# Retention attention with a soft mixture of experts on one core: other first loads, an earlier start of the scores of steps 2 and 3, and another last dispatch

## The chip, the cores and the metric

The kernel runs on one core of one Trainium2 chip. The metric is the device time of one execution in microseconds (us). Before the change it is 166.42 us, the median of three runs (166.32 to 166.59). All data are 32-bit floats, and a 32-bit product on TensorE shows in the trace as two instructions, a transpose as one.

## The reference

Two stages follow each other.

```
attention, per batch b (4) and head h (8), over 768 tokens t, head size 64:
    state = gamma[h] * state + outer(k[t], v[t])
    y[t]  = (q[t] @ state) / sqrt(64)
x = y as [3072 tokens, 512]
logits    = x @ phi                                  # 32 slots, 4 for each of 8 experts
d         = softmax of logits over the TOKENS        # dispatch
slot_in   = d.T @ x                                  # [32, 512]
slot_out  = relu(slot_in[e] @ w1[e]) @ w2[e]         # per expert, hidden size 1024
c         = softmax of logits over the SLOTS         # combine
out       = c @ slot_out
```

The dispatch softmax runs over all 3072 tokens, so no expert can begin before the attention of every token is done.

## The kernel before

**Work units.** The 768 tokens of a batch are cut in 6 chunks of 128. A step is one chunk of one batch: 24 steps, numbered chunk by chunk, step `i` belonging to batch `i % 4`. Two steps make a pair `P` (12 pairs), four steps make a group `g` (6 groups). The state recurrence is written by chunks: inside a step `score_mm` forms k·q for the 8 heads (16 products), `score_mask` (VectorE, one instruction for each of two PSUM banks) masks it into a tile A, and `attend_mm` multiplies it with v. `carry_mm` adds what the running state gives, `state_mm` and `state_add` bring the state forward. The decay factors are multiplied into q and v by GpSimd (`decay_q`, `decay_v`). The first four steps have no earlier state: they skip `carry_mm` and `decay_q`.

**Per pair.** `attend_mm` writes a pair's outputs in banks Y0 and Y1, each holding half of the heads of both steps. `attend_copy` takes them to memory as yT (Y0 by ScalarE, Y1 by VectorE; 128x512 each). `natural_mm` transposes yT (8 transposes), `natural_copy` brings the result to a tile xn. `logits_mm` multiplies yT with phi.

**Per group.** `logits` takes the maximum over the tokens so far and exponentiates; `turn_mm` transposes; `dispatch_u` multiplies the weights with xn, and `dispatch_acc` adds the product to `acc` with the factor `al` for a risen maximum, and to the sum `zrun`. `combine_a`, `combine_b`, `split_c`, `transpose_c` and `copy_c` prepare c.

**The last group** stands apart: its logits have a maximum of their own, and its product `u` is copied by ScalarE (four 128x128 copies), not added to `acc`. Two factors per slot (`wj`, two columns) then bring both to one scale, and the slot inputs `sp` are two rows of four products: one with `acc` (L511), one with `u` (L517). `siT` (L520) is what `hidden` (L533), the first expert product, reads.

**Order and queues.** Every engine executes its instructions in the order in which the program lists them. All transfers are issued by SyncE's queue in order. An input step is one transfer of 1024 KB (k, q, v and k again in token order), but steps 0 and 1 come in three parts: k and q (512 KB), v (256 KB), and k in token order as a late part (256 KB). Steps 0 to 5 are loaded ahead, step `i + 6` when the slot of step `i` is free, that is after `state_mm` of its pair.

**Weights.** 32 weight tiles of 1024 KB go between the inputs by `PACE`. 13 slots of their own and the 6 input slots hold 19 of them. The twentieth waits until `hidden(0, 0)` has used up the first tiles. Twelve output tiles of 512 KB end the program.

**PSUM.** The banks have names: A0 to A3, Y0, Y1, S and sm. `warm` issues products of zeros.

The start, as the program lists it for TensorE (lines 410 to 468): 5 `warm`, `score_mm(0)`, 4 `warm`, `attend_mm(0, [0])`, `score_mm(1)`, 2 `warm`, then pair 0: `attend_mm(0, (1,))`, `state_mm(0)`, `natural_mm(0)`, `score_mm(2)`, `score_mm(3)`, then pair 1: `attend_mm(1)`, `state_mm(1)`, and so on.

Of the kernel before, what the change touches and what calls it, by code (L numbers as in the profile page):

```python
# [80 lines left out]
def retention_soft_moe_kernel(  # L81
# [42 lines left out]
    wsel = small("wsel", [128, 2, NSLOT])  # L124
# [88 lines left out]
    def carry_mm(P):  # L213
        p = pr[P] = dict(Y=[bank(f"Y{b}").rearrange("p (i g t) -> p i g t", i=2, t=C) for b in range(2)])
        if P < B // 2:
            return
        for k in range(2):
            s = st[2 * P + k]
            for gl in range(2):
                for b in range(2):  # L220
                    g = 2 * b + gl
                    for r in range(2):
                        nc.tensor.matmul(p["Y"][b][half(half_of(r, g)), k, gl, :], sst[(2 * P + k) % B][half(r), g, :],  # L223
                                         s["qT"][half(r), g, :], start=(k == 0 and gl == 0), stop=False,
                                         skip_group_check=True)

    def attend_mm(P, ks=(0, 1)):
        for k in ks:
            s = st[2 * P + k]
            for g in range(NPAIR):  # L230
                for r in range(2):
                    nc.tensor.matmul(pr[P]["Y"][g // 2][half(half_of(r, g)), k, g % 2, :], s["v"][:, 2 * g + r, :],  # L232
                                     s["A"][:, r, g, :], start=(P < B // 2 and k == 0 and g % 2 == 0), stop=True,
                                     skip_group_check=True)

    def attend_copy(P):
# [29 lines left out]
    def natural_mm(P):  # L266
        pr[P]["X"] = [bank(f"A{2 + k}") for k in range(2)]
        for k in range(2):
            for g in range(NPAIR):
                nc.tensor.transpose(pr[P]["X"][k][:, g * 128:(g + 1) * 128], pr[P]["yT"][:, k, g, :], ident)  # L270

    def natural_copy(P, engines=("scalar", "scalar")):
        xn = slot()
        for k in range(2):
            st[2 * P + k]["xn"] = xn[:, k * 512:(k + 1) * 512]
            (nc.scalar.copy if engines[k] == "scalar" else nc.vector.tensor_copy)(st[2 * P + k]["xn"], pr[P]["X"][k])  # L276
# [13 lines left out]
    def logits(g):  # L290
# [4 lines left out]
        if g == NGRP - 1:  # L295
            nc.vector.tensor_reduce(nmc[:, 1:2], lt, AX.X, ALU.max, negate=True)
# [38 lines left out]
    def dispatch_u(g, name):  # L335
        q = gs[g]
        q["up"] = bank(name)
        for j in range(GRP):
            nc.tensor.matmul(q["up"][32 * j:32 * j + 32, :], q["p"][:, 32 * j:32 * j + 32], st[GRP * g + j]["xn"],  # L339
                             start=True, stop=True, skip_group_check=True, tile_position=(0, 32 * j))  # L340

    def dispatch_acc(g):
        q = gs[g]
        if g == 0:
            nc.scalar.copy(acc, q["up"])
# [72 lines left out]
    warm(2)  # L418
    decay_table(qtab, K_QT)
    for P in range(NPP):  # L420
# [8 lines left out]
        if not last:  # L429
# [6 lines left out]
            if P == 0:  # L436
# [4 lines left out]
        if P > 0:  # L441
            carry_mm(P)
        if last:
            dispatch_u(g - 1, "A0")
            logits_mm(g, (0, 1))
        attend_mm(P, (1,) if P == 0 else (0, 1))
# [11 lines left out]
        if P % 2 == 1:  # L458
            if g > 0:
                dispatch_u(g - 1, "A0")  # L460
                combine_b(g - 1)
            logits_mm(g, range(GRP))
            if g > 0:
# [9 lines left out]
        if P == NPP - 2:  # L473
            split_c(0)

    weight_pool[0] = big
    dispatch_acc(g - 1)
# [8 lines left out]
    nj = small("nj", [128, 2, GRP])  # L486
    nc.vector.tensor_tensor(nj, nmc.unsqueeze(2).broadcast_to([128, 2, GRP]),
                            kt[:, K_J:K_J + GRP].unsqueeze(1).broadcast_to([128, 2, GRP]), ALU.mult)
    natural_copy(NPP - 1, ("vector", "scalar"))
    copy_c(0, 1)  # L490
    mb = bank("A1", (128, 2 * GRP))
    nc.tensor.matmul(mb, rep, nj.rearrange("p c j -> p (c j)"), start=True, stop=True)
    dispatch_p(g)
    nms = small("nms", [128, 1])
    nc.vector.tensor_reduce(nms, mb, AX.X, ALU.min)
    wj = small("wj", [128, 2])
    nc.scalar.activation(wj, nmc, AF.Exp, bias=nms, scale=-1.0)
    nc.vector.tensor_tensor(wsel, rep[:, 0:NSLOT].unsqueeze(1).broadcast_to([128, 2, NSLOT]),
                            wj.unsqueeze(2).broadcast_to([128, 2, NSLOT]), ALU.mult)
    zw = small("zw", [128, 2])  # L500
    nc.vector.tensor_tensor(zw, zc, wj, ALU.mult)
    warm(1, "A0", 128)
    dispatch_u(g, "Y1")
    dispatch_acc(g)
    sp = bank("A3", (128, NK * NSLOT)).rearrange("p (k s) -> p k s", s=NSLOT)
    zp = bank("S", (128, NSLOT))
    for c in range(2):
        nc.tensor.matmul(zp, zw[:, c:c + 1].broadcast_to([128, 128]), rep[:, 0:NSLOT],
                         start=(c == 0), stop=(c == 1))
    for k in range(NK):  # L510
        nc.tensor.matmul(sp[:, k, :], acc[:, k * 128:(k + 1) * 128], wsel[:, 0, :], start=(k == 0), stop=False,  # L511
# [178 lines left out]
```

## Time and profile before

| what | before |
|---|---|
| median of 3 runs | 166.42 us |
| the profiled execution, its time | 166.58 us |
| its span (first to last instruction) | 164.7 us |
| TensorE busy / weight loads | 149.6 us (91%) / 110.8 us (67%) |
| VectorE, ScalarE, GpSimd busy | 84.6, 39.7, 57.4 us |
| read from and written to HBM | 58.00 MB, 6.29 MB; 390 GB/s over the span |
| the chain that ended last, by engine | TensorE 74%, DMA 12%, SyncE's queue 3%, VectorE 2%, ScalarE 1% |

Columns of the page are shares of the span of the one profiled execution. A timeline row gives the start, the duration, the engine, the line and the operation, what it writes and reads, how many instructions were merged into the row, and in brackets how long the engine had been idle and what ended that. The chain of waits gives start, duration and what held the end at that moment. [...]

### The profile page before, as it was taken

The page shows a single profiled execution, that of the slowest core. Times are in us where ns is not written, and L with a number is a line of the kernel's source. Part 1 is how long each engine was busy: PE and PEld are TensorE (multiplying, and loading weights), DVE is VectorE, ACT ScalarE, POOL GpSimd, SP SyncE. Part 2 cuts the span into 40 slices and gives each one's busy share as a digit, 9 for nine tenths or more (in the row PEclk, how much of TensorE's full clock was granted, in tenths as well). Part 3 has the DMA queues.
Part 4 walks back from the last instruction along what each step waited for, and adds up shares of the span by engine and source line. Part 5 has one row for each costly group of instructions (what it writes and reads, how often), then busy time and mean ns, then how long its engine had stood idle before and what let it go on. Part 6 is the DMA issues. An engine that isn't in the chain of part 4 may idle for free.

```text
span 164.7 us, 5430 instructions
## 1 busy us (share of the span) xinstructions
PE 149.6 (91%) x2386; PEld 110.8 (67%) x2386; DVE 84.6 (51%) x193; ACT 39.7 (24%) x93; POOL 57.4 (35%) x62
## 2 busy tenths in 40 slices
PE   8997799999999999999999899999999999997400
PEld 2566798997999799979997788563244667565200
DVE  0456346375747675867576657546410305662600
ACT  3002020614052224123322332522113001432300
POOL 0222774758496665473984640000000000000000
PEclk9999689999999999999999999999999999999965
DMA  5999999999999999999999999976999999999992
GB/s 141 311 406 424 422 422 412 424 420 414 422 418 422 416 418 416 422 412 417 423 409 415 423 420 420 414 306 251 412 428 424 422 424 416 418 362 416 415 420 106
DMA packets 10825, 64.64 MB, mean 392 GB/s; under 512 B 1201, under 2 KB 1585, under 8 KB 4401
## 3 DMA queue, kind: packets, MB, share of 16 engines
q1 hardware_dynamic: 10800, 64.29, 95.7%
q8 instruction: 19, 0.31, 0.8%
q14 instruction: 6, 0.04, 0.1%
HBM read 58.00 MB, written 6.29 MB: 390 GB/s over the span
## 4 chain that ended last, share of the span: by engine, by line
PE 74%; DMA 12%; SPq 3%; DVE 2%; ACT 1%; issue 1%; DVEq 0%; ACTq 0%
PE A L203 13%; PE Y L232 12%; PE A L270 7%; PE A L630 7%; DMA b<-in_x_dram 6%; DMA out_dram<-b 6%; PE Y L223 6%; PE S L255 5%; PE Y L533 4%; PE sm L286 4%; PE A L339 3%; PE A L533 2%; PE S L533 2%; DVE r L210 1%; PE A L392 1%; PE A L612 1%
## 5 line engine op out<-in xcount | busy, mean ns | idle before, releaser
L210 DVE TENSOR_TENSOR r<-A,kt 128x512 f32<-128x512 f32 x48 | 30.0, 683 | 23.2 <-PE A L203 23.2
L189 POOL TENSOR_TENSOR b<-b,qtab 128x512 f32<-128x512 f32 x20 | 25.5, 1275 | 25.3 <-DMA b<-in_x_dram 22.2
L193 POOL TENSOR_TENSOR b<-b,kt 128x512 f32<-128x512 f32 x24 | 24.6, 1043 | 13.7 <-DMA b<-in_x_dram 13.7
L203 PE MATMUL A<-b 64*128 64x128 f32 x384 | 25.5, 281 | 2.0 <-DMA b<-in_x_dram 1.9
L203 PEld LDWEIGHTS A<-b 64*128 64x128 f32 x384 | 22.8, 188 | 5.0 <-issue 3.9
L232 PE MATMUL Y<-r,b 128*64 128x128 f32 x384 | 25.6, 286 | 0.1
L232 PEld LDWEIGHTS Y<-r,b 128*64 128x64 f32 x384 | 22.2, 143 | 3.2 <-issue 2.2
L276 ACT COPY r<-A 128x512 f32<-128x512 f32 x23 | 12.4, 589 | 30.9 <-PE A L270 30.9
L630 PE MATMUL A<-b,r 128*32 128x128 f32 (+1 forms) x384 | 16.3, 311 | 0.8 <-DMA b<-in_w_dram 0.8
L630 PEld LDWEIGHTS A<-b,r 128*32 128x32 f32 x384 | 10.7, 109 | 7.0 <-issue 2.9
L270 PE MATMUL A<-kt,r 128*128 128x128 f32 x96 | 13.1, 280 | 0.6 <-ACT r L246 0.6
L270 PEld LDWEIGHTS A<-kt,r 128*128 128x128 f32 x96 | 10.3, 141 | 1.7 <-ACT r L246 0.8
L255 PE MATMUL S<-b 128*64 128x64 f32 x320 | 11.2, 222 | 0.0
L223 PE MATMUL Y<-b,sst 64*64 64x128 f32 x320 | 11.0, 275 | 0.0
L255 PEld LDWEIGHTS S<-b 128*64 128x64 f32 x320 | 10.8, 138 | 0.0
L247 DVE COPY r<-Y 128x512 f32<-128x512 f32 x10 | 6.9, 691 | 7.5 <-PE Y L232 7.5
L223 PEld LDWEIGHTS Y<-b,sst 64*64 64x64 f32 x320 | 8.6, 132 | 1.2
L369 POOL TENSOR_TENSOR cnat<-cnat,cz 128x128 f32<-128x128 f32 x6 | 2.4, 401 | 18.8 <-DVE cz L368 18.4
L286 PEld LDWEIGHTS sm<-r,phis 128*32 128x32 f32 x192 | 6.2, 110 | 3.3 <-issue 3.3
L533 PE MATMUL Y<-b,siT 128*32 128x512 f32 x64 | 8.2, 597 | 0.0
L374 PE MATMUL sm<-const-float32-0.0 128*1 128x256 f32 x22 | 7.0, 476 | 0.8 <-PEq L678 0.8
L286 PE MATMUL sm<-r,phis 128*32 128x128 f32 x192 | 7.4, 273 | 0.0
(123 smaller groups left out, 147.9 us busy)
## 6 DMA issues: line engine op xcount, KB each, us to landing
b<-in_w_dram SPq DMA_DIRECT2D x32, 1024.0 KB, 16.1
b<-in_x_dram SPq DMA_DIRECT2D x18, 1024.0 KB, 13.2
out_dram<-b SPq DMA_DIRECT2D x12, 512.0 KB, 9.8
b<-in_x_dram SPq DMA_DIRECT2D x4, 768.0 KB, 13.9
b<-in_x_dram SPq DMA_DIRECT2D x2, 512.0 KB, 5.1
b<-in_x_dram SPq DMA_DIRECT2D x4, 256.0 KB, 6.6
kt<-in_consts_dram SPq DMA_DIRECT2D x1, 136.0 KB, 3.8
kt<-in_consts_dram SPq DMA_DIRECT2D x1, 116.0 KB, 6.6
```

Source lines behind the costliest of these rows:

```text
L189: nc.gpsimd.tensor_tensor(q, q, qtab, ALU.mult)
L193: nc.gpsimd.tensor_tensor(v, v, vsc[:, i // B, :].unsqueeze(2).broadcast_to([128, H, D]), ALU.mult)
L203: nc.tensor.matmul(s["sc"][r][:, g, :], s["kT"][half(r), g, :], s["qT"][half(r), g, :], start=True, stop=True, skip_group_check=True)
L210: nc.vector.tensor_tensor(s["A"][:, r], s["sc"][r], mask.unsqueeze(1).broadcast_to([128, NPAIR, C]), ALU.mult)
L223: nc.tensor.matmul(p["Y"][b][half(half_of(r, g)), k, gl, :], sst[(2 * P + k) % B][half(r), g, :], s["qT"][half(r), g, :], start=(k == 0 an ...
L232: nc.tensor.matmul(pr[P]["Y"][g // 2][half(half_of(r, g)), k, g % 2, :], s["v"][:, 2 * g + r, :], s["A"][:, r, g, :], start=(P < B // 2 an ...
L255: nc.tensor.matmul(S_[half(r), k, g, :], s["kn"][:, 2 * g + r, :], s["v"][:, 2 * g + r, :], start=True, stop=True, skip_group_check=True)
L270: nc.tensor.transpose(pr[P]["X"][k][:, g * 128:(g + 1) * 128], pr[P]["yT"][:, k, g, :], ident)
L276: (nc.scalar.copy if engines[k] == "scalar" else nc.vector.tensor_copy)(st[2 * P + k]["xn"], pr[P]["X"][k])
L286: nc.tensor.matmul(q["ltp"][32 * j:32 * j + 32, :], phis[:, p, :], st[GRP * g + j]["yT"][:, p, :], start=(p == 0), stop=(p == NPAIR - 1), ...
L533: nc.tensor.matmul(hp[g][hf][32 * j:32 * j + 32, :], siT[:, k, :], w1t[4 * g + j, k][:, hf * 512:(hf + 1) * 512], start=(k == 0), stop=(k ...
L630: nc.tensor.matmul(op[32 * j:32 * j + 32, :w], hT[fc // 4][:, fc % 4, 4 * g + j, :], t[:, fc * w:(fc + 1) * w], start=(g == 0 and fc == 0) ...
```

## The change

**First loads.** Step 1's k, q and v come as one transfer of 768 KB instead of two. The rest of the constants and step 2 are issued ahead of the two late parts, step 3 right behind these and ahead of phi. The number of bytes is the same.

**Pair 0.** It gets an order of its own: `score_mm(2)` with its mask goes ahead of `attend_mm(0, (1,))`; `score_mm(3)` with its mask goes behind `state_add(0)` and ahead of `natural_mm(0)`, which now uses banks A0 and A1. The 2 `warm` behind `score_mm(1)` are gone, the table `qtab` is made at the end of pair 0, and GpSimd makes `rep` in pair 1 instead of pair 0.

**Last pair.** Its outputs lie in four banks, Y0 and Y1 for step 22, A1 and S for step 23. Each is copied by itself (four copies of 128x256 instead of two of 128x512), and `natural_mm` of step 22 stands ahead of `logits_mm(5, (2, 3))`, that of step 23 behind it. The transposes of `transpose_c` move behind both.

**Last dispatch.** Its maximum is the running one (one more small VectorE instruction, `tensor_scalar` with `min`), its product is made in two halves of 256 columns in Y1 and A1, and `dispatch_acc` adds each half to `acc` with a factor `al` (one more small ScalarE instruction). The copies to `u`, the second row of slot products (L517), one product for the sum, and one `warm` of 128 columns fall away; `wj`, `wsel`, `zw` and `nj` have one column set instead of two. `copy_c` of both halves moves behind `wj` on ScalarE, and `dispatch_z` is a function of its own.

```diff
         if i < 2:
-            nc.sync.dma_start(t[:, 0:1024], in_[i, :, 0:1024])
             if i == 0:
+                nc.sync.dma_start(t[:, 0:1024], in_[i, :, 0:1024])
                 nc.sync.dma_start(kt[:, 0:K_FIRST], consts[:, 0:K_FIRST])
-            nc.sync.dma_start(t[:, 1024:1536], in_[i, :, 1024:1536])
+                nc.sync.dma_start(t[:, 1024:1536], in_[i, :, 1024:1536])
+            else:
+                nc.sync.dma_start(t[:, 0:1536], in_[i, :, 0:1536])
...
+        if P == NPP - 1:
+            for k in range(2):
+                nc.scalar.copy(y[:, k, 0:2, :], pr[P]["y"][k][0])
+                nc.vector.tensor_copy(y[:, k, 2:4, :], pr[P]["y"][k][1])
+            return
...
         if g == NGRP - 1:
-            nc.vector.tensor_reduce(nmc[:, 1:2], lt, AX.X, ALU.max, negate=True)
+            nmx = small("nmx", [128, 1])
+            nc.vector.tensor_reduce(nmx, lt, AX.X, ALU.max, negate=True)
+            nc.vector.tensor_scalar(nmc[:, 1:2], nmx, nmc[:, 0:1], None, ALU.min)
...
-        elif g == NGRP - 1:
-            q["u"] = slot()[:, 0:512]
-            for k in range(NK):
-                ks = slice(k * 128, (k + 1) * 128)
-                nc.scalar.copy(q["u"][:, ks], q["up"][:, ks])
-        else:
-            nc.vector.scalar_tensor_tensor(zrun, zrun, q["al"], q["z"], ALU.mult, ALU.add)
-            nc.vector.scalar_tensor_tensor(acc, acc, q["al"], q["up"], ALU.mult, ALU.add)
+        w = DM // len(q["up"])
+        for h, up in enumerate(q["up"]):
+            a = acc[:, h * w:(h + 1) * w]
+            nc.vector.scalar_tensor_tensor(a, a, q["al"], up[:, 0:w], ALU.mult, ALU.add)
...
     load_in(0)
     load_in(1)
+    nc.sync.dma_start(kt[:, K_FIRST:], consts[:, K_FIRST:])
+    load_in(2)
     for i in range(2):
         nc.sync.dma_start(*st[i]["late"])
-    nc.sync.dma_start(kt[:, K_FIRST:], consts[:, K_FIRST:])
-    load_in(2)
+    load_in(3)
     nc.sync.dma_start(phis, phi)
-    for i in range(3, NIN):
+    for i in range(4, NIN):
...
-    warm(2)
-    decay_table(qtab, K_QT)
...
+        if P == 0:
+            score_mm(2)
+            score_mask(2)
+            attend_mm(0, (1,))
+            attend_copy(0)
+            state_mm(0)
+            state_add(0)
+            score_mm(3)
+            score_mask(3)
+            natural_mm(0, names=("A0", "A1"))
+            natural_copy(0)
+            decay_table(qtab, K_QT)
+            continue
...
+    dispatch_z(g - 1)
     dispatch_acc(g - 1)
-    transpose_c(0, 0, "A1")
-    transpose_c(0, 1, "S")
     attend_copy(NPP - 1)
+    natural_mm(NPP - 1, (0,))
     combine_b(g - 1)
-    copy_c(0, 0)
+    natural_copy(NPP - 1, ks=(0,))
     logits_mm(g, (2, 3))
-    natural_mm(NPP - 1)
+    natural_mm(NPP - 1, (1,))
     logits(g)
...
-    natural_copy(NPP - 1, ("vector", "scalar"))
-    copy_c(0, 1)
+    natural_copy(NPP - 1, ("vector", "vector"), (1,))
+    transpose_c(0, 0, "A0")
...
     dispatch_p(g)
+    al = gs[g]["al"] = small("al", [128, 1])
+    nc.scalar.activation(al, gs[g - 1]["m"], AF.Exp, bias=nmc[:, 1:2], scale=1.0)
+    transpose_c(0, 1, "A2")
...
-    warm(1, "A0", 128)
-    dispatch_u(g, "Y1")
+    dispatch_u(g, ["Y1", "A1"])
     dispatch_acc(g)
+    copy_c(0, 0)
+    copy_c(0, 1)
...
     for k in range(NK):
-        nc.tensor.matmul(sp[:, k, :], acc[:, k * 128:(k + 1) * 128], wsel[:, 0, :], start=(k == 0), stop=False,
+        nc.tensor.matmul(sp[:, k, :], acc[:, k * 128:(k + 1) * 128], wsel, start=True, stop=True,
                          skip_group_check=True)
...
-    for k in range(NK):
-        nc.tensor.matmul(sp[:, k, :], gs[g]["u"][:, k * 128:(k + 1) * 128], wsel[:, 1, :],
-                         start=False, stop=True, skip_group_check=True)
```

## Rows read from the trace of the kernel before

**Rows 1.** Windows: stretches of two us where the rate falls.

```profile
108.00:110.00 2.00, 2.00 (x19) 1.57 (x22) 0.79 (x3) 0.04 (x1) 0.00 (x0) 1.00 0.78 324
110.00:112.00 2.00, 2.00 (x21) 0.47 (x17) 0.79 (x2) 0.00 (x0) 0.00 (x0) 1.00 0.41 172
112.00:114.00 2.00, 2.00 (x19) 0.56 (x19) 1.60 (x4) 0.31 (x1) 0.00 (x0) 1.00 0.54 168
```

**Rows 2.** SyncE's waits: who waited for what, total, times, longest.

```profile
SPq L160 <- PE sm L558: 9.3, 1, 9.3
```

**Rows 3.** Line L160, weight loads 19 and 20: issue, then us to landing.

```profile
L160 SPq DMA_DIRECT2D b<-in_w_dram x1: 332/332/332, 102.3 to 102.3; - x1
...
DMA to landing us min/median/max: 10.8/10.8/10.8
...
L160 SPq DMA_DIRECT2D b<-in_w_dram x1: 328/328/328, 111.8 to 111.8; - x1
...
DMA to landing us min/median/max: 6.5/6.5/6.5
```

**Rows 4.** DMA queues in 15 to 16.2 us, then in 116 to 117.2 us.

```profile
q8 instruction: 1, 0.02, 5.6%
...
q8 instruction: 1, 0.02, 4.8%
```

**Rows 5.** Timeline of GpSimd and TensorE: the start, then two later inputs.

```profile
12.15 1.20 PE L255 MATMUL S<-b 128*64 128x64 f32 x31
13.37 1.04 POOL L193 TENSOR_TENSOR b<-b,kt 128x512 f32<-128x512 f32 x1 [3.17 <-DMA b<-in_x_dram]
14.30 1.16 PE L203 MATMUL A<-b 64*128 64x128 f32 x16
17.28 1.04 POOL L193 TENSOR_TENSOR b<-b,kt 128x512 f32<-128x512 f32 x1 [2.87 <-DMA b<-in_x_dram]
...
34.74 1.28 POOL L189 TENSOR_TENSOR b<-b,qtab 128x512 f32<-128x512 f32 x1 [0.74 <-DMA b<-in_x_dram]
37.20 1.28 POOL L189 TENSOR_TENSOR b<-b,qtab 128x512 f32<-128x512 f32 x1 [1.18 <-DMA b<-in_x_dram]
```

**Rows 6.** Chain of waits: `attend_mm` of pair 1, and of pair 2.

```profile
18.78 3.24 PE Y L232 x32
...
28.01 1.90 PE Y L232 x32
```

**Rows 7.** Windows around the same place: the granted clock.

```profile
14.60:18.00 3.40, 1.51 (x27) 1.35 (x25) 1.29 (x2) 0.45 (x1) 0.72 (x1) 1.00 1.02 417
18.00:21.40 3.40, 3.40 (x36) 3.18 (x34) 1.29 (x2) 0.00 (x0) 2.69 (x6) 0.51 1.01 419
```

**Rows 8.** Timeline of pairs 8 and 9: GpSimd's v, TensorE's `attend_mm`.

```profile
80.62 2.05 POOL L193 TENSOR_TENSOR b<-b,kt 128x512 f32<-128x512 f32 x2
82.74 1.53 PE L232 MATMUL Y<-r,b 128*64 128x128 f32 x24
```

**Rows 9.** Chain of waits, from the last pair to the first expert product.

```profile
102.22 0.59 PE A L392 x4
...
103.25 1.00 PE sm L286 x16
104.25 1.02 PE A L270 x8
...
105.94 1.09 PE Y L339 x8
...
108.54 0.89 PE A L517 x8
109.96 0.92 PE A L533 x8
```

**Rows 10.** Groups of instructions: the two VectorE sizes.

```profile
L264 DVE TENSOR_TENSOR sst<-sst,S 128x256 f32<-128x256 f32 x16 | 6.0, 417 | 1.9 <-PE S L255 1.9
L353 DVE SCALAR_TENSOR_TENSOR acc<-acc,al,A 128x512 f32<-128x512 f32 x4 | 3.0, 744 | 0.0
```

More of the change, by code (lines that the diff above doesn't have):

```diff
@@ L123, in retention_soft_moe_kernel @@
     zrun = zc[:, 0:1]
-    wsel = small("wsel", [128, 2, NSLOT])
+    wsel = small("wsel", [128, NSLOT])
     siT = small("siT", [128, NK, NSLOT])
@@ L213, in carry_mm @@
     def carry_mm(P):
-        p = pr[P] = dict(Y=[bank(f"Y{b}").rearrange("p (i g t) -> p i g t", i=2, t=C) for b in range(2)])
+        p = pr[P] = {}
+        names = (("Y0", "Y1"), ("A1", "S")) if P == NPP - 1 else (("Y0", "Y1"),)
+        p["Y"] = [bank(n).rearrange("p (i g t) -> p i g t", i=2, t=C) for pair in names for n in pair]
+        p["y"] = [[p["Y"][b][:, k] if P < NPP - 1 else p["Y"][2 * k + b][:, 0] for b in range(2)] for k in range(2)]
         if P < B // 2:
@@ L222, in carry_mm @@
                     for r in range(2):
-                        nc.tensor.matmul(p["Y"][b][half(half_of(r, g)), k, gl, :], sst[(2 * P + k) % B][half(r), g, :],
-                                         s["qT"][half(r), g, :], start=(k == 0 and gl == 0), stop=False,
-                                         skip_group_check=True)
+                        nc.tensor.matmul(p["y"][k][b][half(half_of(r, g)), gl, :], sst[(2 * P + k) % B][half(r), g, :],
+                                         s["qT"][half(r), g, :], start=(gl == 0 and (k == 0 or P == NPP - 1)),
+                                         stop=False, skip_group_check=True)
     def attend_mm(P, ks=(0, 1)):
@@ L264, in state_add, with natural_mm, natural_copy @@
                 nc.vector.tensor_tensor(d, d, pr[P]["S"][:, k], ALU.add)
-    def natural_mm(P):
-        pr[P]["X"] = [bank(f"A{2 + k}") for k in range(2)]
-        for k in range(2):
+    def natural_mm(P, ks=(0, 1), names=("A2", "A3")):
+        X = pr[P].setdefault("X", {})
+        for k in ks:
+            X[k] = bank(names[k])
             for g in range(NPAIR):
[L270 to L276, printed above, removed]
+                nc.tensor.transpose(X[k][:, g * 128:(g + 1) * 128], pr[P]["yT"][:, k, g, :], ident)
+    def natural_copy(P, engines=("scalar", "scalar"), ks=(0, 1)):
+        if "xn" not in pr[P]:
+            pr[P]["xn"] = slot()
+        for k in ks:
+            xn = st[2 * P + k]["xn"] = pr[P]["xn"][:, k * 512:(k + 1) * 512]
+            (nc.scalar.copy if engines[k] == "scalar" else nc.vector.tensor_copy)(xn, pr[P]["X"][k])
     gs = {}
@@ L333, in dispatch_p, with dispatch_u, dispatch_z @@
         nc.vector.tensor_copy(q["p"], pp)
-    def dispatch_u(g, name):
+    def dispatch_u(g, names):
         q = gs[g]
[L337 to L340, printed above, removed]
+        q["up"] = [bank(n) for n in names]
+        w = DM // len(names)
+        for h, up in enumerate(q["up"]):
+            for j in range(GRP):
+                nc.tensor.matmul(up[32 * j:32 * j + 32, 0:w], q["p"][:, 32 * j:32 * j + 32],
+                                 st[GRP * g + j]["xn"][:, h * w:(h + 1) * w], start=True, stop=True,
+                                 skip_group_check=True, tile_position=(0, 32 * j))
+    def dispatch_z(g):
+        q = gs[g]
+        nc.vector.scalar_tensor_tensor(zrun, zrun, q["al"], q["z"], ALU.mult, ALU.add)
     def dispatch_acc(g):
@@ L459, in retention_soft_moe_kernel @@
             if g > 0:
-                dispatch_u(g - 1, "A0")
+                dispatch_u(g - 1, ["A0"])
                 combine_b(g - 1)
             logits_mm(g, range(GRP))
+            if g > 1:
+                dispatch_z(g - 1)
             if g > 0:
@@ L489, in retention_soft_moe_kernel @@
-    natural_copy(NPP - 1, ("vector", "scalar"))
-    copy_c(0, 1)
-    mb = bank("A1", (128, 2 * GRP))
-    nc.tensor.matmul(mb, rep, nj.rearrange("p c j -> p (c j)"), start=True, stop=True)
+    nj = small("nj", [128, GRP])
+    nc.vector.tensor_scalar(nj, kt[:, K_J:K_J + GRP], nmc[:, 1:2], None, ALU.mult)
+    natural_copy(NPP - 1, ("vector", "vector"), (1,))
+    transpose_c(0, 0, "A0")
+    mb = bank("S", (128, GRP))
+    nc.tensor.matmul(mb, rep, nj, start=True, stop=True)
     dispatch_p(g)
+    al = gs[g]["al"] = small("al", [128, 1])
@@ L501, in retention_soft_moe_kernel @@
-    nc.vector.tensor_tensor(zw, zc, wj, ALU.mult)
-    warm(1, "A0", 128)
-    dispatch_u(g, "Y1")
+    wj = small("wj", [128, 1])
+    nc.scalar.activation(wj, nmc[:, 1:2], AF.Exp, bias=nms, scale=-1.0)
+    gs[g]["z"] = zc[:, 1:2]
+    dispatch_z(g)
+    nc.vector.tensor_scalar(wsel, rep[:, 0:NSLOT], wj, None, ALU.mult)
+    zw = small("zw", [128, 1])
+    nc.vector.tensor_tensor(zw, zrun, wj, ALU.mult)
+    dispatch_u(g, ["Y1", "A1"])
     dispatch_acc(g)
+    copy_c(0, 0)
+    copy_c(0, 1)
@@ L505, in retention_soft_moe_kernel @@
+    zp = bank("S", (128, NSLOT))
+    nc.tensor.matmul(zp, zw.broadcast_to([128, 128]), rep[:, 0:NSLOT], start=True, stop=True)
     sp = bank("A3", (128, NK * NSLOT)).rearrange("p (k s) -> p k s", s=NSLOT)
[L506 to L509, printed above, removed]
     for k in range(NK):
-        nc.tensor.matmul(sp[:, k, :], acc[:, k * 128:(k + 1) * 128], wsel[:, 0, :], start=(k == 0), stop=False,
+        nc.tensor.matmul(sp[:, k, :], acc[:, k * 128:(k + 1) * 128], wsel, start=True, stop=True,
```

24 lines of the change are left out of this document (9 added, 15 removed).

## The prediction, made before the changed kernel was run

> **What bounds the kernel now.** I read the slices first: TensorE is 91% busy, and the DMA engines are at nine tenths or more in nearly every slice, so either could be the bound. Windows of two microseconds then show where the transfers slacken [rows 1]: at 108 to 114 us they run at 324, 172 and 168 GB/s; in full stretches they run near 420 (417 and 419 in [rows 7]). The loss is (3 x 420 - 324 - 172 - 168) x 2 / 420 = 2.84 us of full rate. SyncE's waits say why [rows 2]: once, for 9.3 us, a weight load waits for TensorE. It is the twentieth tile, which needs the first tiles used up by `hidden(0, 0)`. That product begins at 109.96 us in the chain of waits [rows 9], where TensorE leads from 17 us to there. So the end is a sum of two things: transfers that never pause except in this hole, and the moment at which TensorE reaches `hidden(0, 0)`, which ends the hole. What TensorE gains before 109.96 us counts, but only up to what the hole holds.
>
> How much it holds is not 2.84 us, which is a mean over 16 engines, since a load is there only when its slowest part is. Weight 19 lands at 102.3 + 10.8 = 113.1 us, weight 20 at 111.8 + 6.5 = 118.3 us [rows 3]: 5.2 us apart. Where the queue never runs dry, inputs of the same size come 37.20 - 34.74 = 2.46 us apart [rows 5]. The hole therefore costs at most 5.2 - 2.46 = 2.7 us. Part of this may not be hole: around 116 us one packet of instructions runs in these engines [rows 4], 4.8% of 16 engines over 1.2 us, 0.92 us of one engine. The same kind of packet at 15 to 16.2 us (5.6%, 1.08 us) lies in the only long early gap, 17.28 - 13.37 = 3.9 us between steps 2 and 3 [rows 5], 1.3 us more than 2.46 and phi's 0.15. If the slowest engine meets such a packet again, the hole gives back only 2.7 - 1.3 = 1.4 us.
>
> **The start.** Step 2 lands by 13.37 us and step 3 by 17.28 us [rows 5]. The change puts the two late parts (512 KB) behind step 2, at 2.46 us per 1024 KB worth 1.2 us: step 2 at 12.1 us. Step 3 has ahead of it what it had, less phi (64 KB, 0.15 us). The merged load of step 1 saves between nothing (the bytes are the same) and 0.6 us (its v, 256 KB, as if free: a quarter of 2.46); I take 0.2, about the one issue of 0.33 us [rows 3] that goes. Step 1's scores now wait for its v too, by the same 0.6 us at most, and this vanishes in the wait for step 2, which `score_mm(2)` now imposes on all that is queued behind it: `attend_mm(0, (1,))`, `state_mm(0)`, and by that VectorE's copies, SyncE's load of step 6 (behind steps 4 and 5 and a weight in the transfers, so nobody waits) and GpSimd's later inputs. The 2 `warm` filled that place; now TensorE idles there for about 2 us.
>
> From 11.9 us: `score_mm(2)` 1.16 [rows 5], half an `attend_mm` 0.95 [rows 6], `state_mm` about 1.2 [rows 5]: 15.2 us. Then comes the wait for step 3. Two outcomes follow, and I price both.
>
> (a) Step 3 lands before the instruction packet, at 17.28 - 0.15 - 0.2 - 1.3 = 15.7 us. Then `score_mm(3)` 1.16, `natural_mm(0)` 1.02 (the size in rows 9) and `attend_mm(1)` 1.90 end at 19.8 us. [...] TensorE would be 2.2 us early.
>
> (b) The packet comes first again: step 3 at 16.9 us, an idle time of 1.7 us, about as long as before (1.89 us), and the clock falls at 18 us as it did. Behind the landing stand 1.16 + 1.02 + 1.90 = 4.08 us of work, and the low stretch of 3.4 us does half of its share, 1.7 us lost: 22.7 us, 0.7 us later than before. The edit's own cost is here: `natural_mm(0)`, 1.02 us, now stands behind the landing instead of ahead of it.
>
> Which one? In the row at 14.30 us `score_mm(2)` has begun [rows 5], and the packet falls between 15 and 16.2 us, when some ten of its 16 instructions or all of them had been taken [rows 4]. After the change TensorE stops for step 3 with 12 instructions fewer behind it than at the end of that row (4 of `warm`, 8 transposes), so at a place that it had passed before the packet came. If its progress calls the packet, the packet now comes after step 3; if the time does, (b) holds. [...]
>
> In (a) not all of the 2.2 us arrive. GpSimd takes each input as it lands, and its landings depend on the transfers, not on TensorE. The tightest place is pair 9: v of step 19 is ready at 80.62 + 2.05 = 82.67 us [rows 8], and the second half of `attend_mm(9)` begins at 82.74 + 0.95 = 83.7 us. A lead beyond 1.0 us is lost there; with some of the merged load's 0.2 I keep 1.1 us. `rep` in pair 1 and `qtab` behind the third mask cost nothing: GpSimd then waits for steps 6 and 4 anyway.
>
> **The tail.** From the end of `attend_mm(11)`, 102.22 us, to 109.96 us the chain takes 7.74 us [rows 9]. Step by step: with banks of their own, step 22's copies run while step 23's products are made, so `natural_mm` of step 22 (0.51) follows at once, and `logits_mm` begins at 102.73 instead of 103.25: 0.5 us early. The added `min` on VectorE lies on the path, and VectorE also takes the second `natural_copy`, ahead of the copy of the transposed weights; I take 0.2 for it, between nothing (under TensorE's transposes) and 0.7 (a whole 128x512 copy). `dispatch_u` thus begins at 105.6 instead of 105.94, and its two halves last the same 1.09: 106.7. Its second half must now be added by VectorE before the last two slot products: between 0.42 (a 128x256 operation) and 0.74 (the 128x512 accumulation) [rows 10], and I take 0.45, nearest to its own width: 107.2. ScalarE's copies to `u` had hidden under the first row of products. The two slot products left after this are 0.45, and the last `warm` is 109.96 - 108.54 - 0.89 = 0.53: with three handovers of about 0.05 that gives 108.4 us. The second product row (0.89) and one product for the sum are what goes; the four small copies of 128x256 cost VectorE more than the two large, but beside TensorE. So 109.96 - 108.4 = 1.5 us, from 0.7 (both high ends) to 1.7.
>
> **Sum.** In (a) TensorE reaches `hidden(0, 0)` 1.1 + 1.5 = 2.6 us early and the hole decides: 1.4 to 2.7 us, plus 0.2 of the merged load. Since packets recur, I take the low end: 1.4 + 0.2 = 1.6 us. The profiled execution took 166.58 us (span 164.7 and 1.9 around it), 0.16 above the median, so 165.0 for it and 164.8 for the median.
>
> **The rivals.**
> - (b), the clock falls again: 1.5 - 0.7 = 0.8 us, under the hole's limit: 165.6 us. For it: an idle time as long as before. Against it: the order of packet and landing.
> - The hole gives everything: 2.7 + 0.2 us, 163.5 us. For it: the lead of 2.6 us suffices. Against it: the packet near 116 us.
> - The hole gives nothing: the slowest engine was still at weight 19 until 113.1 us, 1.3 us after weight 20 was issued, so an earlier issue may find it busy. Then 166.2 us (the 0.2 of the merged load alone), no change. Against it: the 5.2 us between the landings, which one packet doesn't fill.
> - Slower: the low clock lasts for two stretches at the start, since two idle times now follow each other (2 us before step 2, up to 1.7 before step 3). Each low stretch after step 3's landing costs 1.7 us: -0.7 - 1.7 + 1.5 = -0.9, which moves `hidden(0, 0)` and the hole's end later: 167.3 us. It decides when `attend_mm(1)` ends later than 23.5 us. Against it: the clock came back after one stretch when TensorE had work.
>
> **How the numbers follow.** What this kernel's measurement tells from no change is about 0.2%, 0.33 us. Chances: the forecast 0.46, (b) 0.24, everything 0.06, nothing 0.14, slower 0.10. Faster is the first three: 0.76; same 0.14; slower 0.10. The range leaves out half of "everything" (0.03), the slower case (0.10), and a part of "nothing" that lies above 166.4 (0.06): 163.6 to 166.4 us.
>
> **What would show it.** Right: step 3's scores begin before 16 us; the granted clock stays at 1.00 from 18 to 21.4 us; `hidden(0, 0)` begins at 107.4 us or earlier with about 6.2 us from the last `attend_mm` to it; the rate at 108 to 114 us has no hole. Wrong: `attend_mm(1)` ends after 22 us; the lead at pair 11 is under zero; or the hole is gone and the end has not moved, which would mean that the slowest engine sets it.

## The result, and the profile after

The changed kernel takes 165.11 us in the median of 20 executions (164.22 to 165.89), the kernel before 166.62 in 20 (165.27 to 168.93): a ratio of 0.9911, 95% interval 0.9886 to 0.9935. Ratios leave out executions more than 1.5% above the shortest of their kernel, such as the 168.93 us here. The profiled executions took 164.77 and 166.58 us. The forecast was 164.8 (165.0 for the profiled one). The sum came out right; several of its terms did not.

The start went as outcome (a). Windows of the changed kernel (stretch, length, busy us of PE, PEld, DVE, ACT and POOL, granted clock of TensorE as a share of its full speed, DMA share, GB/s), the lines that answer to [rows 7] and [rows 1]:

```profile
14.60:18.00 3.40, 2.16 (x38) 1.93 (x33) 2.19 (x5) 0.00 (x0) 1.04 (x1) 1.00 1.02 413
18.00:21.40 3.40, 3.40 (x71) 3.17 (x69) 2.68 (x6) 1.07 (x2) 1.28 (x1) 1.00 1.02 424
...
108.00:110.00 2.00, 2.00 (x18) 0.50 (x16) 1.18 (x3) 0.00 (x0) 0.00 (x0) 1.00 0.85 352
110.00:112.00 2.00, 2.00 (x21) 0.56 (x17) 1.28 (x3) 0.31 (x1) 0.00 (x0) 1.00 0.70 217
112.00:114.00 2.00, 2.00 (x20) 0.84 (x20) 1.62 (x5) 0.59 (x1) 0.01 (x1) 1.00 0.96 373
```

The clock, 0.51 from 18 us in the kernel before, is 1.00, and TensorE does in the second stretch 71 instructions instead of 36. The hole at 108 to 114 us is shallower, and it is still there. SyncE's longest wait for TensorE (answer to [rows 2]) went from 9.3 to 8.0 us:

```profile
SPq L160 <- PE sm L588: 8.0, 1, 8.0
```

Weights 19 and 20 (answer to [rows 3]: issue, then us to landing) land at 102.1 + 10.8 = 112.9 and 110.2 + 6.2 = 116.4 us, 3.5 us apart where it was 5.2:

```profile
L160 SPq DMA_DIRECT2D b<-in_w_dram x1: 331/331/331, 102.1 to 102.1; - x1
...
DMA to landing us min/median/max: 10.8/10.8/10.8
...
L160 SPq DMA_DIRECT2D b<-in_w_dram x1: 327/327/327, 110.2 to 110.2; - x1
...
DMA to landing us min/median/max: 6.2/6.2/6.2
```

The timeline of GpSimd and TensorE (start, us, instruction, idle time before it and releaser; answer to [rows 5]) shows the scores of steps 2 and 3 starting right behind the landings of these steps, after waits of 1.20 and 1.24 us:

```profile
11.84 1.04 POOL L195 TENSOR_TENSOR b<-b,kt 128x512 f32<-128x512 f32 x1 [1.75 <-DMA b<-in_x_dram]
11.91 1.16 PE L205 MATMUL A<-b 64*128 64x128 f32 x16 [1.20 <-DMA b<-in_x_dram]
16.20 1.04 POOL L195 TENSOR_TENSOR b<-b,kt 128x512 f32<-128x512 f32 x1 [3.31 <-DMA b<-in_x_dram]
16.27 0.94 PE L205 MATMUL A<-b 64*128 64x128 f32 x12 [1.24 <-DMA b<-in_x_dram]
```

The chain of waits (start, us, engine, tile, line; answers to [rows 6] and [rows 9]):

```profile
18.45 1.90 PE Y L237 x32
...
101.99 0.59 PE A L281 x4
102.58 1.00 PE sm L298 x16
...
105.56 0.59 PE Y L355 x8
106.14 0.43 PE A L355 x8
106.57 0.34 PE S L541 x2
106.91 0.91 PE A L544 x8
107.82 0.52 PE A L392 x2
108.35 1.02 PE A L563 x8
```

`attend_mm(1)` takes 1.90 us at a granted clock of 1.00 where it took 3.24 at 0.58 in the mean (0.50 until 21.5 us), and ends at 20.35 us instead of 22.02. The last pair's products end at 101.99 instead of 102.22, only 0.23 us earlier; the tail from there to the first expert product is 6.36 us instead of 7.74. So in this profile 1.38 of the 1.61 us were gained in the last eight microseconds before that product, although TensorE had been 1.7 us ahead at pair 1.

### The profile page after: what moved, and what is told of

It is laid out like the page before. It is cut to its first block, busy times and chain, and to the rows that moved or that the text cites. A ratio compares the mean times of both kernels' runs of the same rounds, so it can differ in the third digit from the quotient of the medians.

```text
span 163.0 us, 5416 instructions
## 1 busy us (share of the span) xinstructions
PE 146.4 (90%) x2378; PEld 108.4 (67%) x2378; DVE 88.2 (54%) x198; ACT 39.1 (24%) x91; POOL 57.5 (35%) x62
## 4 chain that ended last, share of the span: by engine, by line
PE 62%; DMA 22%; SPq 3%; DVE 2%; POOL 2%; issue 2%; ACT 1%; DVEq 0%; ACTq 0%; POOLq 0%
DMA b<-in_x_dram 16%; PE A L205 10%; PE Y L237 9%; PE A L660 7%; PE A L281 6%; DMA out_dram<-b 6%; PE Y L563 4%; PE Y L228 4%; PE S L265 4%; PE sm L298 3%; PE A L563 2%; PE S L563 2%; PE A L355 2%; PE A L410 2%; DVE r L212 2%
## 5 line engine op out<-in xcount | busy, mean ns | idle before, releaser
L237 PE MATMUL Y<-r,b 128*64 128x128 f32 x368 | 23.0, 276 | 0.0
L237 PEld LDWEIGHTS Y<-r,b 128*64 128x64 f32 x368 | 19.8, 137 | 2.5 <-issue 2.0
L257 DVE COPY r<-Y 128x512 f32<-128x512 f32 x9 | 6.2, 690 | 5.9 <-PE Y L237 5.9
L379 ACT ACTIVATE cnat<-cnat 128x128 f32<-128x128 f32 x6 | 1.9, 310 | 23.0 <-DVE cnat L378 23.0
```

What stands on the lines that cost most here:

```text
L237: nc.tensor.matmul(pr[P]["y"][k][g // 2][half(half_of(r, g)), g % 2, :], s["v"][:, 2 * g + r, :], s["A"][:, r, g, :], start=(P < B // 2 an ...
```

## The experiments

The table has one profile of each of fourteen runs. Wait: TensorE's idle time before `score_mm(3)`. Clock: granted from 18.0 to 21.4 us. Lead: how much earlier than in the first profile of the kernel before the first score product of pair 1 (step 4) and of pair 9 (step 20) begins. Hidden: the first expert product in the timeline. Gap: between the landings of weights 19 and 22. Last: landing of the last transfer. us: time of the profiled execution; median: of all executions of that run. Ratio: to the kernel before on the same chip, 95% interval.

```
kernel                           wait clock  lead  lead  hidden   gap   last    us      median  ratio
                                             pair1 pair9
before                           1.89  0.51   -     -    109.82   9.90  163.64  166.58  166.62
before again (e12)               1.86  0.60  0.03 -0.04  109.86   9.73  163.40  166.36  -
changed                          1.24  1.00  1.68  0.35  108.30   8.51  162.00  164.77  165.11  0.991 [0.989, 0.994]
changed again (e7_again)         1.20  1.00  2.07  1.17  107.48   7.70  161.76  164.67  165.28  0.992 [0.990, 0.995]
start only (e1)                  1.56  1.00  1.14 -1.27  111.09   9.92  164.96  167.73  166.28  0.997 [0.994, 1.000]
loads only (e4)                  none  1.00  1.28 -0.32  110.14   9.77  163.87  166.65  166.23  0.996 [0.993, 0.999]
tail only (e2)                   1.96  0.53 -0.08 -0.21  108.86   8.43  162.19  165.03  165.09  0.988 [0.984, 0.992]
changed, two banks (e9)          1.86  0.58 -0.13 -0.87  110.06   9.02  163.58  166.50  165.57  0.994 [0.991, 0.997]
accumulate first (e3)            1.18  1.00  1.88  1.04  107.60   7.93  161.50  164.38  165.06  0.989 [0.984, 0.994]
the same again (e7_accfirst)     3.39  0.50 -2.94 -3.06  111.71  10.61  165.55  168.33  164.53  0.987 [0.983, 0.991]
and loads ahead of weights (e8)  1.03  1.00  1.95  1.72  106.93   8.26  161.24  164.02  164.79  0.989 [0.985, 0.994]
and step 3 in two pieces (e11)   0.17  1.00  2.93  2.73  105.92   7.46  161.48  164.33  164.43  0.986 [0.983, 0.989]
no late v scaling (e6)           1.88  0.62 -0.67 -1.15  109.79   8.06  163.15  165.93  -
step 3 late (e10)                1.74  1.00  1.00  0.41  108.24   8.41  161.87  164.71  165.91  0.994 [0.991, 0.998]
```

Two profiled executions were the longest of their run: that of e7_accfirst (seven executions) and that of e1 (twelve, 1.45 us above its median). Their rows stand for these executions, not for the medians.

**Which part carries the gain.** Four kernels: the new start (loads and pair 0) on the kernel before; the new loads alone; the changed kernel with the old start (loads and pair 0); and the changed kernel with the last pair's outputs in two banks.

e1_start: the kernel before with (cut)

```
+            else:
+                nc.sync.dma_start(t[:, 0:1536], in_[i, :, 0:1536])
...
+    load_in(2)
     for i in range(2):
         nc.sync.dma_start(*st[i]["late"])
...
+    load_in(3)
...
+        if P == 0:
+            score_mm(2)
...
+            score_mm(3)
+            score_mask(3)
+            natural_mm(0, names=("A0", "A1"))
```

> The kernel before with the first loads and the order of pair 0 of the change, and its old last pair and last dispatch. Theory A (the loop follows the landings): TensorE is some 1.7 us early behind pair 1, and this lead is gone by pair 7 down to the 0.3 us by which the inputs land earlier, since in odd pairs small VectorE instructions wait behind GpSimd, and the next scores wait for VectorE; so hidden(0,0) begins 0.2 to 0.4 us early and the time falls by 0.2 to 0.4 us. Theory B (the lead is kept to about 1 us, as predicted): hidden(0,0) about 1.1 us early, the time 0.9 to 1.2 us lower.

e2_tail: the changed kernel with the first loads and the order of pair 0 as before.

> The changed kernel with the first loads and the order of pair 0 as before; only the last pair's banks and the last dispatch are changed. Theory A: 6.4 us instead of 7.7 from the last attend_mm to hidden(0,0), 1.4 us early, and the time 1.2 to 1.4 us lower than before, nearly all of what the whole change gives. Theory B: the same 1.4 us, but then the two parts alone add up to more than the 1.5 us of the whole, because the hole limits the sum.

Measured: 0.997 for the start alone, 0.988 for the tail alone, and 0.991 and 0.992 for both. The start alone has its clock at 1.00 and a lead of 1.14 us at pair 1; at pair 5 it is 0.46, at pair 9 -1.27. The tail alone has no lead at any place, a tail of 108.90 - 102.54 = 6.36 us in its chain of waits, and the whole gain:

```profile
102.54 0.59 PE A L279 x4
...
108.90 1.02 PE A L550 x8
```

By the ratios the two parts alone give 0.3% and 1.2%, together more than the 0.9% of both, which is theory B of e2_tail. The intervals leave this open, since those of the parts add up to anything from 0.8 to 2.2%. For the start alone they fit theory A (0.2 to 0.4 us) and do not quite exclude the 0.9 us of theory B.

e4_loads: the kernel before with the loads of e1_start, the order of pair 0 as it was.

> The kernel before with the first loads of the change alone, the order of pair 0 as it was. Theory (what the start gives is step 3's landing, not the order of TensorE's work): step 3 lands near 16.1, the clock stays at 1.00 from 18 to 21.4 us, lead near 1 us at pair 1, less than 0.5 at pair 10, tail 7.6 us, and the time within 0.3% of the kernel before. Rival (the order of pair 0 is what counts): lead 0.3 us or less at pair 1.

Measured: 0.996 [0.993, 0.999], a gain no smaller than with the order of pair 0. Step 3 lands at 16.78 us, before TensorE needs it; with the order of before TensorE is busy up to there, and the clock stays at 1.00. The lead is 1.28 us at pair 1 and gone at pair 7. The rival (the order counts, a lead of 0.3 us or less at pair 1) is out.

e9_twobanks:

```
-        names = (("Y0", "Y1"), ("A1", "S")) if P == NPP - 1 else (("Y0", "Y1"),)
+        names = (("Y0", "Y1"),)
...
-        if P == NPP - 1:
-            for k in range(2):
-                nc.scalar.copy(y[:, k, 0:2, :], pr[P]["y"][k][0])
-                nc.vector.tensor_copy(y[:, k, 2:4, :], pr[P]["y"][k][1])
-            return
```

> The changed kernel with the last pair's outputs in two banks as before, all else as in the change. Theory (the banks carry half of the shorter tail): the copies can only start when both steps are done, the first transposes wait for VectorE's copy of 128x512 and start near 102.8 in place of 102.0, the tail is 7.15 in place of 6.36 us, and the time is 0.8 us above the changed kernel. Rival (the dispatch added to the rest carries it all): tail 6.4 us and the changed kernel's time.

In its chain of waits the copy of 128x512 on VectorE stands between the last output product and the first transpose, as forecast:

```profile
103.15 0.70 DVE r L252
103.85 0.04 issue
103.89 0.44 PE A L276 x2
...
110.11 1.02 PE A L558 x8
```

From the products' end, 103.12, the tail is 6.99 us (7.15 expected): the four banks carry 0.63 of the 1.38 us, and 0.75 remains for all else that changed behind the last pair, the new last dispatch above all, which no run has alone. The median was 165.57 us beside 165.28 for the changed kernel, 0.3 higher, with overlapping intervals, and in the profile a start with low clock adds to it. So the 0.63 us is shown by the chain; the 0.8 us expected of the time is not shown.

**Where the lead of the loop went.** In the changed kernel TensorE is 1.68 us ahead until pair 5, 0.9 behind it, 0.38 behind pair 7. The timeline there (VectorE and GpSimd, pair 5):

```profile
52.97 2.04 POOL L195 TENSOR_TENSOR b<-b,kt 128x512 f32<-128x512 f32 x2
53.11 0.93 DVE L385 TENSOR_SCALAR cz<-cz 128x4 f32<-128x4 f32 x1
54.07 0.18 DVE L386 RECIPROCAL cz<-cz 128x4 f32<-128x4 f32 x1
54.16 0.86 DVE L361 SCALAR_TENSOR_TENSOR zc<-zc,al,z 128x1 f32<-128x1 f32 x1
54.95 0.73 DVE L371 SCALAR_TENSOR_TENSOR acc<-acc,al,A 128x512 f32<-128x512 f32 x1
...
55.78 0.46 PE L205 MATMUL A<-b 64*128 64x128 f32 x3 [0.81 <-POOL cnat L387]
```

GpSimd's two v instructions run from 52.97 to 55.01. VectorE's operation on 128x4 elements takes 0.93 us and ends with the first; the one on 128x1 takes 0.86 and ends with the second. Only then comes the accumulate, which reads bank A0, and `score_mm(12)`, which writes A0, 0.1 us after it (the instruction named in brackets, begun at 54.97 us and 0.40 us long, was done 0.4 us earlier: the accumulate is the one that fits). The order of the two starts goes with it: the 128x4 operation, begun 0.14 us behind GpSimd's, takes 0.93 us; begun ahead of it, 0.17 (below, in the second profile of the changed kernel). By what means GpSimd holds it up is not shown.

e3_accfirst puts the accumulate, which frees the bank, ahead of the small operations:

```
                 dispatch_u(g - 1, ["A0"])
+                dispatch_acc(g - 1)
                 combine_b(g - 1)
...
-            if g > 0:
-                dispatch_acc(g - 1)
```

> The changed kernel; in odd pairs VectorE adds the dispatch product to acc at once, ahead of the small instructions of combine_b and of the sum zrun, so that bank A0 is free for the next scores without waiting for them. Theory A: the lead of TensorE no longer falls at pairs 5 and 7; hidden(0,0) begins up to 1 us earlier than in the changed kernel (108.35 us), and since the landings of weights 19 and 20 there are still 3.6 us apart instead of 2.5, the time falls by 0.4 to 1.0 us more. Theory B (the hole was the limit): hidden(0,0) may come earlier, the time stays within 0.2 us of the changed kernel.

Its timeline at the same place: the accumulate, with one operand in PSUM, takes 0.75 us beside GpSimd, and `score_mm(12)` begins 0.97 us earlier than in the changed kernel.

```profile
52.97 2.04 POOL L195 TENSOR_TENSOR b<-b,kt 128x512 f32<-128x512 f32 x2
53.96 0.75 DVE L371 SCALAR_TENSOR_TENSOR acc<-acc,al,A 128x512 f32<-128x512 f32 x1 [1.29 <-PE A L355]
...
54.81 0.94 PE L205 MATMUL A<-b 64*128 64x128 f32 x12
54.94 0.17 DVE L385 TENSOR_SCALAR cz<-cz 128x4 f32<-128x4 f32 x1
55.15 0.18 DVE L386 RECIPROCAL cz<-cz 128x4 f32<-128x4 f32 x1
55.24 0.19 DVE L361 SCALAR_TENSOR_TENSOR zc<-zc,al,z 128x1 f32<-128x1 f32 x1
```

The lead is kept through pair 7 (1.88 us) and is 1.04 us at pair 9. e6_nov takes GpSimd's part away (`decay_v` returns at once from step 8 on: the later steps' v are not scaled):

> The changed kernel without decay_v on GpSimd for steps 8 to 23: v stays unscaled there, so this part of the computation is left out. Theory A: the small VectorE instructions of odd pairs (the sum in combine_b at 0.68 to 0.93 us, the zrun update at 0.86 us) come down to 0.15 to 0.25 us, and TensorE keeps a lead of more than 1 us over the kernel before until pair 9. If something else takes the lead (the landings themselves, or a bank), these instructions or the lead stay as they are.

There the two small operations take 0.24 and 0.20 us in the mean, where the changed kernel has 0.48 and 0.70: GpSimd is what they wait for. What this does to the lead can't be read from it, since its step 3 came late (16.88 us) and the lead was below zero from pair 1 on.

The changed kernel and e3 once more, on one chip with the next two:

> The changed kernel once more, on the chip of the next three, as their yardstick. If the start lands as in the first profile (step 3 before 16.3 us) the granted clock stays at 1.00 from 14.6 to 21.4 us, TensorE is 1.7 us ahead of the kernel before at pair 1 and keeps some 0.35 of it, the tail from the last output product to the first hidden product is 6.35 us, and the time is near 165. If step 3 lands after 16.8, as it did in the kernel without the later v scaling, the clock of 18 to 21.4 falls to about 0.6 and the lead is -0.7, with a time near 166.

> The changed kernel with the accumulate ahead of combine_b, again, now beside the changed kernel. Theory (the last transfer follows the first hidden product at a fixed distance of about 53.6 us as long as the hole among the weights is not filled): 0.5 to 0.9 us below the changed kernel in the median. Rival (the loop's lead is worth nothing, since the stream of transfers sets the end): within 0.2 us of it.

The second profile of the changed kernel kept its lead through pair 8. At pair 5 everything was a little earlier, and one of the two small operations escaped:

```profile
52.71 0.17 DVE L385 TENSOR_SCALAR cz<-cz 128x4 f32<-128x4 f32 x1
52.81 2.05 POOL L195 TENSOR_TENSOR b<-b,kt 128x512 f32<-128x512 f32 x2
...
53.01 0.86 DVE L361 SCALAR_TENSOR_TENSOR zc<-zc,al,z 128x1 f32<-128x1 f32 x1
53.80 0.73 DVE L371 SCALAR_TENSOR_TENSOR acc<-acc,al,A 128x512 f32<-128x512 f32 x1
54.63 2.06 PE L205 MATMUL A<-b 64*128 64x128 f32 x32
...
78.00 1.27 POOL L191 TENSOR_TENSOR b<-b,qtab 128x512 f32<-128x512 f32 x1 [1.20 <-DMA b<-in_x_dram]
79.32 0.94 PE L205 MATMUL A<-b 64*128 64x128 f32 x12 [0.50 <-POOL b L191]
```

It lost its lead later, at 78 to 79.3 us: step 19 lands at 77.87, GpSimd scales its q, and `score_mm(19)` waits for that. What was left, 1.17 us, is close to the prediction's 1.1. So the lead is taken back in two ways, by the small operations or by landings, and which one differs from one execution to the next. The profiled e7_accfirst shows a third: there step 3 landed at 18.03 us, TensorE waited 3.39 us, the clock stayed at 0.50 up to 24 us, and the lead was -2.94 us. In medians the kernel of e3 was at 165.06 and 164.53 us, the changed kernel at 165.11 and 165.28; what the reorder gives in time, between 0.05 and 0.75 us, can't be told from nothing by these intervals.

e8_swap, on top of e3:

```
-        load_weights(PACE[P])
         if 2 * P + NIN < NSTEP:
             load_in(2 * P + NIN)
             load_in(2 * P + NIN + 1)
-        else:
+        load_weights(PACE[P])
+        if 2 * P + NIN >= NSTEP:
             weight_pool[0] = inp
```

> The same with the loads of each pair's next two steps ahead of its weights. Theory: inputs' landings capped the lead that was left, so the steps from pair 5 on land 2.5 us earlier, the lead stays at 1.9 us to the last pair, the first hidden product starts near 106.8, three us ahead of before; the hole among the weights is then filled (0 where the kernel before had 2.45 us), so the stream sets the end and no more than 0.5 us comes out beside the kernel with only the reorder. Rival 1 (landings do not cap): lead and time as in the kernel with only the reorder. Rival 2 (TensorE still sets the end): 0.9 us below it.

Measured: the lead is 1.95 us to pair 8 and 1.72 at pair 9, where e3 has 1.04, so landings were the cap. The first expert product is 0.67 us earlier than in e3, the last transfer 0.26, and the median, 164.79, no lower than that of e3's kernel on the same chip, 164.53. Rival 2 (0.9 us below) is out. The hole was smaller but, against the expectation, not quite filled: the transfers still fell to 344 GB/s at 110 to 112 us, and the gap is 8.26 us.

**The clock.** e10_late3 makes step 3 late (cut):

```
-    load_in(3)
+    t3, t4 = large(inp), large(inp)
+    nc.sync.dma_start(t4[:, 0:768], in_[4, :, 0:768])
+    load_in(3, t3)
...
+    load_in(4, t4, 768)
```

> The changed kernel with step 3 made late: the first 768 columns of step 4 are loaded ahead of it, so that it lands some 0.9 us later, near 17. Theory (the wait of score_mm(3) decides the clock of the next stretch, and TensorE's lead reaches the end): granted clock 0.5 to 0.65 from 18.0 to 21.4 us, lead over the kernel before -0.5 to -0.9 us at pair 1 in place of +1.7 to +2.1, first hidden product 0.9 to 2.4 us later than in the changed kernel, time 0.5 to 0.9 us above it. Rival (the loop gives the lead back whatever it is, by its landings): the same clock, but the time within 0.2 us of the changed kernel's 165.1 to 165.3.

Step 3 landed at 16.81 us, 0.7 later than in the changed kernel, and the clock, against the expectation, did not fall. The window of e10, and that of e9, whose step 3 landed earlier, at 16.37:

```profile
18.00:21.40 3.40, 3.40 (x62) 3.20 (x62) 2.65 (x5) 1.07 (x2) 1.28 (x1) 1.00 1.00 417
```

```profile
18.00:21.40 3.40, 3.40 (x30) 3.07 (x30) 1.63 (x3) 1.17 (x2) 1.27 (x1) 0.58 1.01 424
```

So the time of the landing doesn't decide it. What sorts the fourteen profiles is TensorE's wait for step 3: with 0.17 to 1.74 us (and none) in eight of them the stretch was granted 1.00; with 1.86 to 3.39 us in six it was granted 0.50 to 0.62, with 0.50 for most of it. The idle time ahead of step 2 does not sort them: e10, which kept its clock, waited there for 1.47 us besides, the kernel before not at all. No run sets the wait alone, so that it is the cause is not shown. The median was 165.91 us, 0.9943 [0.9908, 0.9978], 0.6 us above the changed kernel's on that chip; the profiled execution, without the fall, took 164.71 like the changed kernel's. Whether the others had the fall isn't seen, so the price of the late landing in time stays open.

e12_before, the kernel before again:

> The kernel before once more, for a second profile. Where its clock falls again between 18 and 21.4 us, everything stands as in the first. Where it does not, theory 1 (the odd pairs give a lead back): TensorE is some 1.2 us ahead of the first profile at pair 1, no more than 0.4 us ahead at pair 10, and the time is within 0.4 us of 166.5. Theory 2 (a lead lasts): 1.2 us ahead at pair 10 and a time near 165.4.

Its clock fell again, and all stands as in the first profile within 0.14 us to the first expert product. So it says nothing about the two theories, which asked for a profile without the fall.

**How much the hole holds.** e11_short3, on top of e8, loads step 3 without its last quarter first (cut):

```
-        if i < 2:
+        if i < 2 or i == 3:
...
     nc.sync.dma_start(phis, phi)
+    nc.sync.dma_start(*st[3]["late"])
```

> The changed kernel with the accumulate ahead of combine_b, the loads ahead of the weights, and step 3 in two pieces, its last quarter after the table phi, so that what score_mm(3) needs lands near 15.5. Theory (with the hole filled the stream sets the end): lead 2.3 us at pair 1 and at least 1.7 at pair 10, clock 1.00 throughout, hole none, last transfer 48.5 us or a little more after weight 19 as in the kernel without the last edit, and the median at most 0.3 us below that kernel's 164.8. Rival (TensorE still sets the end): 0.5 us below it or more.

TensorE starts step 3 at 15.02 us, almost without a wait, and the lead is 2.73 us at pair 9. The first expert product is 3.9 us earlier than in the kernel before, and the hole has gone:

```profile
108.00:110.00 2.00, 2.00 (x18) 0.53 (x18) 1.51 (x4) 0.31 (x1) 0.00 (x0) 1.00 0.95 381
110.00:112.00 2.00, 2.00 (x20) 0.85 (x24) 1.40 (x4) 0.58 (x1) 0.39 (x1) 1.00 1.03 430
112.00:114.00 2.00, 2.00 (x24) 0.59 (x20) 1.12 (x2) 0.58 (x1) 0.01 (x1) 1.00 0.99 414
```

Weights 19 to 22 land in 7.46 us, three times 2.49. In the kernel before it was 9.90: the hole held 2.44 us. This version has the lowest ratio of all, 0.9859 [0.9825, 0.9893], 164.43 us in the median of 6; the interval touches the changed kernel's first one (0.9886 to 0.9935) at its edge. The median lies 0.36 us below e8's, between what the theory allowed (0.3) and what the rival asked for (0.5), so the times do not decide between them. The last transfer does, in one profile each: e11's first expert product is 1.01 us earlier than e8's, its last transfer 0.24 later, and from weight 19 to the last transfer it is 48.40 us beside 48.49.

The table shows the law behind it. From the first expert product to the last transfer it is 53.3 to 53.9 us in the eleven profiles where that product begins at 107.6 us or later: a microsecond of TensorE is about one of the time. It is 54.28, 54.31 and 55.56 in the three that come earlier (107.48, 106.93, 105.92): there the transfers begin to set the end, and of what TensorE still gains, part is lost in e8 and all in e11.

## Why the prediction was right, point by point

The forecast of the time was met partly by luck: two terms were off by about a microsecond each, in opposite directions. Of the signs that it named for being right, the first profile shows one, the clock at 1.00; step 3's scores began at 16.27 us (before 16), `hidden(0, 0)` at 108.35 (107.4 or earlier), and the hole was still there. None of the signs for wrong came.

- **What bounds the kernel**: right. End = first expert product + 53.6 us until the hole is full.
- **Step 2 and the merged load**: step 2 landed at 11.8 us (11.9 in the prediction); weight 19 came 0.24 us earlier (0.2), which proves nothing for the merged load: in e4, with the same loads, it came 0.09 us later than in the kernel before.
- **Step 3**: outcome (a) held, its reason did not. The prediction let the packet of instructions come behind the landing. The packet began at 15.47 us, 0.44 after TensorE's last product ahead of the wait had ended, so ahead of the landing; step 3 still landed 2.54 us after the load ahead of it, at 16.13, and not at 15.7, and the wait was 1.24 us instead of 0.5 (15.7 less 15.2). The clock was 1.00, as the lengths behind the 19.8 us of (a) need. The lead was 1.7 instead of 2.2 us (22.02 less 19.8). (b) is as real: with the same start, e6 and e9 had it, and e6's -0.67 us at pair 1 agrees with the -0.7 worked out for it, e9's -0.13 does not. That TensorE's progress calls the packets, on which the choice of (a) rested, was the author's estimate, and no run had shown it. The later packets agree with it: that near 103.9 us in the kernel before came at 102.98 in e7_again (lead 1.17) and at 101.45 in e11 (2.73). For the first packet no run settles what calls it: in the four profiles with the order of before it began 0.65 to 0.83 us behind the start of `score_mm(2)`, in e4 too, where that product came 1.6 us later; in the ten with the new order it began 0.12 to 1.22 us behind the end of `state_mm(0)`.
- **What arrives of the lead**: mis-sized. "A lead beyond 1.0 us is lost there; with some of the merged load's 0.2 I keep 1.1 us" (pair 9) was right in size, 1.17 in the second profile, where step 19 is waited for by its q and not, as argued, by its v. In the first only 0.35 arrived (0.23 at the end of the last products), because VectorE's small operations waited for GpSimd in pairs 5 and 7 (0.93 and 0.86 us, then 0.68 and 0.86) and held bank A0. The prediction had looked at GpSimd's v alone, not at what it does to VectorE; in the kernel before the same was to be seen (0.32 us mean for the 128x4 operation whose undisturbed time is 0.17).
- **The tail**: 1.38 us instead of 1.5. `natural_mm` followed the products at once, as said; the two halves of the dispatch ended 4.58 us after the products instead of 4.5, and the slot products 5.83 instead of 5.4. The halves of the accumulate took 0.48 us each (0.45), but they are not what stands in the chain: there TensorE makes the product for the sum (L541, 0.34) and all four slot products (L544, 0.91), 1.25 us, where the prediction had the second half's accumulate and two slot products, 0.9.
- **The hole**: "the hole decides: 1.4 to 2.7 us" failed in the first profile. TensorE brought 1.6 us, not 2.6, so TensorE decided, and of the hole 8.51 - 7.46 = 1.05 us was left. In the second profile it brought 109.82 - 107.48 = 2.34 us, of which 163.64 - 161.76 = 1.88 arrived, with 0.24 us of the hole left: there the forecast's picture nearly held. The reason for the low end, a packet near 116 us that fills part of the gap, did not come true in e11: it emptied the hole by 2.44 us, with the packet at 114.06 us in the time of weight 20, which still landed 2.49 us behind weight 19. In other executions packets may cost something (last section). Two errors of about one microsecond, TensorE's gain too high and the hole too small, cancelled: 1.6 forecast, 166.58 - 164.77 = 1.81 us in the profiled executions.
- **The slower rival** came in one profile, by one long wait for step 3 (3.39 us) instead of two in a row: e7_accfirst, 168.33 us (167.3 in the prediction).

## What to carry to other kernels

When an end is the sum of a compute chain and a stream with one hole, write down the fixed distance from the chain's event to the last transfer in every profile: here it held within 0.6 us while the chain was the bound, and grew where the stream was. Shorten a chain at its end before its start: the 1.4 us after the last point where inputs pace the loop arrived whole, of the 1.1 to 2.1 us at the start between nothing and 1.2 us did. An operation that frees a buffer for the bottleneck should stand ahead of small operations that another engine can hold up: here they took up to 0.93 us instead of 0.17, and with the accumulate ahead of them `score_mm(12)` began 0.97 us earlier.

## What the runs showed of the hardware that was not expected

- The two small VectorE operations, on 4 and on 1 elements per partition and all in SBUF, take 0.17 and 0.19 us alone and up to 0.93 beside a GpSimd instruction of 1.02 us; in e4 the mean of the first was 0.68 us. The reduce (0.28 us beside GpSimd), the reciprocal (0.18) and the accumulate that reads PSUM (0.73 to 0.75) were not stretched.

```profile
L369 DVE TENSOR_SCALAR cz<-cz 128x4 f32<-128x4 f32 x6 | 4.1, 681 | 0.2
```

- The landing of one load, step 3, varied from 15.73 to 18.03 us over eight profiles with the same start, and TensorE's wait for it from 1.03 to 3.39 us. Late landings go with packets of instructions: over the fourteen profiles, of 58 loads of steps and weights that landed more than 2.75 us behind the load ahead of them, though issued 2 us or more before that one's landing, 54 had such a packet in this time; of 622 that landed 2.3 to 2.75 us behind, 257 had. A packet takes about 1 us (0.92 and 1.08 in [rows 4]), and most delay nothing; that it is the cause where a load is late is not shown.
